# Attention and two expert layers on one core: later softmax sums as reductions with a constant column, an early softplus table, planner constants, and the last output chunk in halves

## The chip, the cores and the metric

The kernel runs on one core of a Trainium2 chip. Its time is the device time of one execution in microseconds; of several runs the median counts. The engines are TensorE (PE in the profile, its weight loads PEld), VectorE (DVE), ScalarE (ACT), GpSimd (POOL) and SyncE (SP), which issues the transfers.

## The reference

Attention over a window of 64 positions is followed by two expert layers, one with softplus and one with a gate.

```python
def _attn_ref(q, k, v):                       # B 4, H 8, S 576, D 64, window 64
    ...
    scores = np.where(mask, scores, -1000000000.0)
    scores = scores - np.max(scores, axis=-1, keepdims=True)
    attn = np.exp(scores)
    attn = attn / (np.sum(attn, axis=-1, keepdims=True) + 1e-09)
    return np.matmul(attn, v).astype(np.float32)

def _moe_ref(x, w_in, w_out):                 # 2304 tokens, 512 -> 2048 -> 512
    h = x @ w_in
    g = np.maximum(h, 0.0) + np.log1p(np.exp(-np.abs(h)))
    return (g @ w_out).astype(np.float32)

def _moe2_ref(x, w_gate, w_val, w_out):       # 2304 tokens, 512 -> 1536 -> 512
    gate = 1.0 / (1.0 + np.exp(-(x @ w_gate)))
    val = x @ w_val
    return (gate * val @ w_out).astype(np.float32)
```

## The kernel before

**Precision.** Every operand of a matmul is kept as a high part (a cast) and a low part (the value less its cast), and a product is three matmuls: high by high, high by low, low by high. So each intermediate result needs a cast on ACT and a subtraction on DVE or POOL before PE can use it. Weights arrive as 64-bit floats and are decoded on the way: `w_load` (L146, a DMA), `w_scale` (L175 or L177, ACT), `w_shift` (L181, DVE), `w_sign` (L186, DVE), `w_low` (L191, DVE), `w_hi` (L197, a cast on ACT) and `w_lo` (L205, DVE or POOL). Where the planner gives `w_scale` the form with Prelu (L175), that also sets the sign, and `w_sign` falls away.

**Stages.** The 2304 tokens are 36 groups of 64 rows. The attention of the first eight groups ("near") is the lead-in, before M1. M1 is the softplus layer in five token blocks of 512, 384, 384, 512 and 512, each with 16 tiles f of the hidden dimension: `m1_proj(b, f)` (L514, twelve matmuls into bank h0 or h1, by f), `m1_act` (L531, softplus on ACT), `g_hi` (L538, ACT), `g_lo` (L544, DVE), and two tiles later `m1_out(b, f)` (L491 to L493, twelve matmuls). Each `m1_proj` or `m1_out` is a slot of PE, some 2.7 us at 512 columns. The attention of block b+1 ("far" in the notes below: all groups from the ninth on) is done during M1 of block b: `att_scores` of a pair of groups (L335, PE), `att_max` (L364, L367, DVE), `att_exp` (L381, ACT, four exponentials of 128x128 with a sum of each row), `att_sum` (L389, L390, DVE), `att_norm` (L397, POOL), then for block 1 `att_transpose` on PE (L413) and `att_copy` (L448), for the later blocks a transpose on DVE and a round trip through DRAM, and at last `att_values` (L474, PE) with its split (L482, L487). M2, the gated layer, follows with its own slots, and ends with `m2_out` (L491 to L493) and `m2_store` (L687 to L694).

**Order.** All engines work in program order. Up to M2 that order comes from `lead_in()`, a list scheduler: of all steps that are ready and could begin within `NEAR` us (`SLACK` after `OPEN`) of the soonest it takes the one with the lowest rank. It works with a table of estimated durations, with the time `OPEN` at which M1 is thought to begin, with `RG` as the distance of two near groups in slots, and with `FETCH`, a time about which it expects transfers to pause. ACT holds one table of functions at a time: exponentials and softplus lie in different ones, and a switch is an `ACT_TABLE_LOAD`. The compiler puts such a load ahead of the first instruction that needs it, and what that instruction waits for is then waited for by the load.

Of the kernel before, what the change touches and what calls it, by code (L numbers as in the profile page):

```python
# [10 lines left out]
F32 = mybir.dt.float32  # L11
# [3 lines left out]
AF = mybir.ActivationFunctionType  # L15
ALU = mybir.AluOpType
AX = mybir.AxisListType
# [3 lines left out]
P = 128  # L21
# [5 lines left out]
FAR = 2  # L27
MERGE = 8
SHIFTED = 2,
RG = 1.2  # L30
HURRY = 1.5
SLACK, NEAR = 0.1, 0.2
STAY = 10.0
FETCH, PAUSE, SAFE = 15.5, 1.4, 0.4
OPEN = 30.0
FLYING, SWITCH, MARGIN, FLIP, LATE = 10, 1.3, 1.1, 8, 0.5
EITHER, HALVES = (("pool", 1.29), ("dve lock", 0.69)), (("pool", 0.75), ("dve lock", 0.42))
COPIES = ("act", 0.55), ("dve", 0.69)
# [10 lines left out]
STB, PB, VB, GB, RB = 3, 2, 2, 3, 2  # L49
# [3 lines left out]
def tile_kernel(ctx: ExitStack, tc: tile.TileContext, qk, vt, w1, w2, wg, wv, wo, out):  # L53
# [20 lines left out]
    nc = tc.nc  # L74
# [8 lines left out]
    NF2 = wg.shape[0]  # L83
    NB1 = len(BLOCKS1)
    N1 = NMAX = max(BLOCKS1)
    NS2 = NT // (2 * HALF)
    NCH = 2 * HALF // P
# [13 lines left out]
    early = main.tile([P, 2, DM], BF16, tag="sums", name="early", bufs=1)  # L101
    ident16, mask16 = (early[:, k, :P] for k in range(2))
    sums = early[:, 0, P:2 * P].bitcast(F32).rearrange("p (g j two) -> p g j two", j=4, two=2)
    x2d = dram.tile([KC, P, NT], F32, tag="x2d", name="x2d")
    wcd = [dram.tile([P, 14 * HC], F32, tag=f"wcd{f}", name=f"wcd{f}") for f in range(NF2)]
    pd = [dram.tile([4, 32, 4, P], F32, tag=f"pd{i}", name=f"pd{i}") for i in range(2)]
# [263 lines left out]
    def att_bias(g, engine):  # L370
        t = st_t[g][:, 0, :]
        eng = nc.gpsimd if engine == "pool" else nc.vector
        eng.tensor_scalar(out=t, in0=t, scalar1=SCALE, scalar2=None, op0=ALU.mult)

    def att_exp(g):
        w = width(g)
        p, st = p_t[g], st_t[g]
        s, scale = ([p[:, j] for j in range(NPAIR)], 1.0) if g >= NG0 else (
            [s_t[g][:, h, j] for h in range(s_t[g].shape[1]) for j in range(NPAIR // s_t[g].shape[1])], SCALE)
        for j in range(NPAIR):  # L380
            nc.scalar.activation(out=p[:, j, :w], in_=s[j][:, :w], func=AF.Exp, bias=st[:, 0, j:j + 1], scale=scale,  # L381
                                 accum_out=sums[:, g, j, :1] if g < NG0 else st[:, 1, j:j + 1])

    def att_sum(g):
        st = st_t[g]
        if g < NG0:
            nc.vector.tensor_reduce(out=st[:, 1, :], in_=sums[:, g], axis=AX.X, op=ALU.add)
        else:
            nc.vector.tensor_scalar(out=st[:, 1, :], in0=st[:, 1, :], scalar1=1e-9, scalar2=None, op0=ALU.add)  # L389
        nc.vector.reciprocal(out=st[:, 2, :], in_=st[:, 1, :])  # L390

    def att_norm(g):
# [135 lines left out]

    def m1_act(b, f):
        t = h_t.pop((b, f))  # L530
        nc.scalar.activation(out=t, in_=t, func=AF.Softplus)  # L531
        u_t[b, f] = t

# [131 lines left out]
    def m2_out(s, f, c):  # L665
        if f == 0 and c == 0:
            acc_t[s] = [psum(f"acc{i}") if i < KC else psum("at", 2) for i in range(NCH)]
        g, w = g_t[s, f, c * P // HALF], w_t["wo", f]
        cols = slice(c * P % HALF, c * P % HALF + P)
        mm3(acc_t[s][c], g[:, 0, cols], g[:, 1, cols], w[:, 0, :], w[:, 1, :], f == 0, f == NF2 - 1)  # L670

    y_t = {}

    def m2_store(s, c):
        t0 = 2 * s * HALF + c * P
        if s < NS2 - 1:
            y = main.tile([P, 512], F32, tag="stage", name="y", bufs=STB)
        elif c % 3:
            y = y_t[c - c % 3][:, c % 3]
        else:  # L680
            y_t[c] = main.tile([P, 4, 512], F32, tag="raw", name="y", bufs=RB)
            y = y_t[c][:, 0]
        if s == NS2 - 1 and c == NCH - 1:
            for k, copy in enumerate((nc.vector.tensor_copy, nc.scalar.copy)):
                cols = slice(256 * k, 256 * k + 256)
                y = y[:, cols] if k == 0 else main.tile([P, 512], F32, tag="stage", name="y", bufs=STB)[:, cols]
                copy(out=y, in_=acc_t[s][c][:, cols])  # L687
                nc.sync.dma_start(out=out[t0:t0 + P, cols], in_=y)
            return
        if c % 2:  # L690
            nc.scalar.copy(out=y, in_=acc_t[s][c])
        else:
            nc.vector.tensor_copy(out=y, in_=acc_t[s][c])
        nc.sync.dma_start(out=out[t0:t0 + P, :], in_=y)  # L694
# [93 lines left out]
    for b in range(1, NB1):  # L788
        s0, s1 = pos[m1_proj, b - 1, 0], pos[m1_proj, b, 0]
        ng, g0 = BLOCKS1[b] // Q, starts1[b] // Q  # L790
        for j in range(ng):
            far = b >= FAR
            first = -5 if far else 5
            t = s0 + first + (s1 - s0 - (14 if far else 12 + first)) * (j // 2) // max(ng // 2 - 1, 1)
            attention(g0 + j, t, far)
            at(t - 4, -60, qk_load, g0 + j)
# [72 lines left out]

    def consts():  # L870
        nc.gpsimd.memset(sums, 1e-9)
        make_identity(nc, ident)
        nc.vector.tensor_copy(out=ident16, in_=ident)
        for t, inside, outside in (mask16, 0.0, -1e30), (mask, 3.0e38, -1e9):
            nc.gpsimd.memset(t, inside)
            for h in range(2):
                m = t[h * Q:(h + 1) * Q, :]
                nc.gpsimd.affine_select(out=m, in_=m, pattern=[[1, P]], compare_op=ALU.is_ge, fill=outside, base=-1,
                                        channel_multiplier=-1)
                nc.gpsimd.affine_select(out=m, in_=m, pattern=[[-1, P]], compare_op=ALU.is_ge, fill=outside, base=Q,  # L880
                                        channel_multiplier=1)
# [198 lines left out]
    def lead_in():  # L1080
# [30 lines left out]
        while todo:  # L1111
            ready, other = [], "soft" if table == "exp" else "exp"
            for n, key in enumerate(todo[:AHEAD]):
# [5 lines left out]
                if all(d in done for d in deps + after[key]):  # L1119
                    ends_at, best = [(done[d] - lead(key, d), made[d]) for d in deps], None  # L1120
                    visit = kind == "pe" and key[0] not in (m1_proj, m1_out) and key[1] >= NG0
                    for kind, us in kind if kind in CHOICES else ((kind, us),):
                        engine, *need = kind.split()
                        start = max([t - (0.08 if e == "pe" else 0.05) * (e == engine) for t, e in ends_at], default=0.0)
                        start = max(free[engine], start + LATE * visit)
                        if engine == "pool" or "lock" in need:
                            start = max(start, held["dve" if engine == "pool" else "pool"])
                        if engine == "sp" and len(flying) >= FLYING:
                            start = max(start, flying[-FLYING])
                        if engine == "act" and need and need[0] != table:  # L1130
                            us += SWITCH
                        if best is None or start + us < best[0] + best[2]:
                            best = start, kind, us
                    ready.append((best[0], rank + FLIP * (best[1].split()[-1] == other) - STAY * (visit and stay is key[0]), n, key,
                                  *best[1:]))
# [95 lines left out]
```

## Time and profile before

| | |
|---|---|
| median of 3 runs | 878.88 us (878.85 to 881.1) |
| the profiled execution | 878.93 us |
| its span | 877.1 us |
| PE busy | 868.3 us, 99% |
| DVE busy | 519.4 us, 59% |
| ACT busy | 395.5 us, 45% |
| first matmul of M1 | at 25.14 us |
| last matmul | begins at 872.46 us |

The profile shows one execution. A busy time is the sum of an engine's instructions, and times in the trace count from the start of the span. A wait is the idle time of an engine just ahead of an instruction, with the instruction of another engine that ended it.

### The profile page before, as it was taken

The page shows a single profiled execution, that of the slowest core. Times are in us where ns is not written, and L with a number is a line of the kernel's source. Part 1 is how long each engine was busy: PE and PEld are TensorE (multiplying, and loading weights), DVE is VectorE, ACT ScalarE, POOL GpSimd, SP SyncE. Part 2 cuts the span into 40 slices and gives each one's busy share as a digit, 9 for nine tenths or more (in the row PEclk, how much of TensorE's full clock was granted, in tenths as well). Part 3 has the DMA queues.
Part 4 walks back from the last instruction along what each step waited for, and adds up shares of the span by engine and source line. Part 5 has one row for each costly group of instructions (what it writes and reads, how often), then busy time and mean ns, then how long its engine had stood idle before and what let it go on. Part 6 is the DMA issues. An engine that isn't in the chain of part 4 may idle for free.

```text
span 877.1 us, 14033 instructions
## 1 busy us (share of the span) xinstructions
PE 868.3 (99%) x5307; PEld 775.3 (88%) x5307; DVE 519.4 (59%) x926; ACT 395.5 (45%) x870; POOL 151.1 (17%) x156
## 2 busy tenths in 40 slices
PE   8999999999999999999999999999999999999998
PEld 5787889999999888888889999999999999999997
DVE  5999985547665654555326677667444448444444
ACT  7878766556566763344323333343222225212222
POOL 5001110112000220012002232332111111111110
PEclk9999999999999999999999999999999999999999
DMA  9955647756877747643325755546554445444442
GB/s 363 390 181 207 207 143 269 246 207 211 263 254 261 266 150 269 199 165 132 133 84 208 269 207 216 217 168 240 208 200 160 151 150 209 168 158 168 169 168 73
DMA packets 56563, 177.73 MB, mean 203 GB/s; under 512 B 6128, under 2 KB 21744, under 8 KB 51888
## 3 DMA queue, kind: packets, MB, share of 16 engines
q1 hardware_dynamic: 56496, 176.84, 56.4%
q8 instruction: 42, 0.69, 0.3%
q14 instruction: 25, 0.20, 0.1%
HBM read 139.59 MB, written 37.22 MB: 202 GB/s over the span
## 4 chain that ended last, share of the span: by engine, by line
PE 93%; ACT 3%; DVE 3%; issue 1%; DMA 1%; POOL 0%; SPq 0%; POOLq 0%; DVEq 0%; ACTq 0%
PE h L514 21%; PE acc L491 11%; PE acc L492 11%; PE acc L493 11%; PE h L491 10%; PE h L493 10%; PE h L492 10%; PE at L493 2%; PE at L492 2%; PE at L491 2%; PE at L474 2%; PE at L335 1%; ACT w L381 1%; DMA w<-in_qk 1%; DVE w L186 1%
## 5 line engine op out<-in xcount | busy, mean ns | idle before, releaser
L514 PE MATMUL h<-xt,w 128*128 128x512 f32 (+1 forms) x960 | 211.6, 369 | 0.9 <-DVE g L544 0.7
L620 DVE TENSOR_TENSOR w<-h,w 128x384 f32<-128x384 f32 x216 | 117.1, 556 | 159.9 <-PE h L493 157.0
L514 PEld LDWEIGHTS h<-xt,w 128*128 128x128 f32 x960 | 174.2, 188 | 25.6 <-DVE g L544 0.9
L491 PE MATMUL h<-w,wc 128*128 128x384 f32 x504 | 169.1, 336 | 0.1
L493 PE MATMUL h<-w,wc 128*128 128x384 f32 x504 | 168.9, 335 | 0.0
L492 PE MATMUL h<-w,wc 128*128 128x384 f32 x504 | 168.7, 335 | 0.0
L632 POOL TENSOR_TENSOR g<-w,g 128x384 fp32r<-128x384 f32 x70 | 74.0, 1057 | 297.0 <-ACT g L625 252.1
L491 PE MATMUL acc<-g,w 128*128 128x512 f32 (+1 forms) x320 | 119.4, 373 | 0.0
L492 PE MATMUL acc<-g,w 128*128 128x512 f32 (+1 forms) x320 | 117.7, 368 | 0.0
L493 PE MATMUL acc<-g,w 128*128 128x512 f32 (+1 forms) x320 | 117.7, 368 | 0.0
L544 DVE TENSOR_TENSOR g<-h,g 128x512 fp32r<-128x512 f32 (+1 forms) x80 | 50.8, 636 | 93.9 <-ACT g L538 87.5
L531 ACT ACTIVATE h<-h 128x512 f32<-128x512 f32 (+1 forms) x80 | 43.0, 540 | 124.2 <-PE h L514 122.2
L491 PEld LDWEIGHTS h<-w,wc 128*128 128x128 f32 x504 | 94.6, 188 | 2.7 <-DVE w L620 0.7
L492 PEld LDWEIGHTS h<-w,wc 128*128 128x128 f32 x504 | 94.6, 188 | 2.0
L493 PEld LDWEIGHTS h<-w,wc 128*128 128x128 f32 x504 | 94.6, 188 | 0.0
L625 ACT CAST g<-w 128x384 fp32r<-128x384 f32 x72 | 36.9, 513 | 118.6 <-DVE w L620 118.6
L491 PEld LDWEIGHTS acc<-g,w 128*128 128x128 f32 x320 | 60.1, 188 | 8.9 <-issue 1.0
L493 PEld LDWEIGHTS acc<-g,w 128*128 128x128 f32 x320 | 60.1, 188 | 7.6
L492 PEld LDWEIGHTS acc<-g,w 128*128 128x128 f32 x320 | 60.1, 188 | 7.1
L397 POOL TENSOR_TENSOR p<-p,st 128x512 f32<-128x512 f32 x28 | 30.7, 1099 | 201.0 <-DVE st L390 114.4
L658 ACT ACTIVATE w<-w 128x384 f32<-128x384 f32 x36 | 19.0, 527 | 94.5 <-DVE w L620 94.4
L493 PE MATMUL acc<-w,g 128*128 128x512 f32 x144 | 56.9, 395 | 0.0
(138 smaller groups left out, 1187.6 us busy)
## 6 DMA issues: line engine op xcount, KB each, us to landing
wc<-wcd SPq DMA_DIRECT2D x36, 1792.0 KB, 7.3
qk<-in_qk SPq DMA_DIRECT2D x28, 512.0 KB, 5.5
wcd<-raw SPq DMA_DIRECT2D x24, 512.0 KB, 3.2
w<-in_w SPq DMA_DIRECT2D x16, 512.0 KB, 8.8
raw<-in_w SPq DMA_DIRECT2D x16, 512.0 KB, 4.9
v<-in_vt SPq DMA_DIRECT2D x25, 256.0 KB, 3.2
raw<-in_wg SPq DMA_DIRECT2D x12, 512.0 KB, 5.3
raw<-in_wv SPq DMA_DIRECT2D x12, 512.0 KB, 6.2
```

The lines of the kernel that those rows point to most:

```text
L397: nc.gpsimd.tensor_tensor(out=p[:, j:j + n, :w], in0=p[:, j:j + n, :w], in1=st[:, 2, j:j + n].unsqueeze(2).to_broadcast([P, n, w]), op=ALU ...
L474: nc.tensor.matmul(out=o[h * Q:(h + 1) * Q, j, k * Q:(k + 1) * Q], lhsT=v[r, (2 * j + h) * Q:(2 * j + h + 1) * Q], rhs=pt, start=True, sto ...
L491: nc.tensor.matmul(out=o, lhsT=lh, rhs=rh, start=first, stop=False)
L492: nc.tensor.matmul(out=o, lhsT=lh, rhs=rl, start=False, stop=False)
L493: nc.tensor.matmul(out=o, lhsT=ll, rhs=rh, start=False, stop=last)
L514: nc.tensor.matmul(out=o, lhsT=w[:, i, kc * P:(kc + 1) * P], rhs=x[:, j, kc, :n], start=t == 0, stop=t == len(turns) - 1)
L531: nc.scalar.activation(out=t, in_=t, func=AF.Softplus)
L544: nc.vector.tensor_tensor(out=g[:, 1, :n], in0=t, in1=g[:, 0, :n].bitcast(F32), op=ALU.subtract)
L620: nc.vector.tensor_tensor(out=out, in0=a, in1=b, op=op)
L625: nc.scalar.copy(out=g[:, 0, :HALF], in_=t)
L632: eng.tensor_tensor(out=g[:, 1, :HALF], in0=t, in1=g[:, 0, :HALF].bitcast(F32), op=ALU.subtract)
L658: nc.scalar.activation(out=sb, in_=u2, func=AF.Sigmoid)
```

## The change

Four parts, and the constants of the planner.

- The sums of the exponentials of the later groups go to a new tile `far_sums`, whose second column holds 1e-9 throughout, and are added up with it by a `tensor_reduce`, as the first eight groups have it already. Before, 1e-9 was added by a `tensor_scalar`.
- The softplus table is asked for by an instruction of its own ahead of the first softplus; the planner lets that step begin 1.3 us (`SWITCH`) earlier.
- The last `m2_out` chunk is done in two halves of 256 columns, three matmuls each. Its two copies are swapped between ACT and DVE, write into one tile, and one transfer of 512 columns sends it.
- The constants change, and block 1's attention is asked for from slot 6 of M1 on, not from slot 5.

```diff
-RG = 1.2
+RG = 1.1
-SLACK, NEAR = 0.1, 0.2
+SLACK, NEAR = 0.15, 0.1
-FETCH, PAUSE, SAFE = 15.5, 1.4, 0.4
-OPEN = 30.0
+FETCH, PAUSE, SAFE = 12.8, 1.4, 0.4
+OPEN = 31.0
...
+    far_sums = main.tile([P, 3, 4, 2], F32, tag="far_sums", name="far_sums", bufs=1)
...
+    def sum_row(g):
+        return sums[:, g] if g < NG0 else far_sums[:, g % 3]
...
-                                 accum_out=sums[:, g, j, :1] if g < NG0 else st[:, 1, j:j + 1])
+                                 accum_out=sum_row(g)[:, j, :1])
...
-        if g < NG0:
-            nc.vector.tensor_reduce(out=st[:, 1, :], in_=sums[:, g], axis=AX.X, op=ALU.add)
-        else:
-            nc.vector.tensor_scalar(out=st[:, 1, :], in0=st[:, 1, :], scalar1=1e-9, scalar2=None, op0=ALU.add)
+        nc.vector.tensor_reduce(out=st[:, 1, :], in_=sum_row(g), axis=AX.X, op=ALU.add)
...
+        if b + f == 0:
+            nc.scalar.preload_act_table(AF.Softplus)
         nc.scalar.activation(out=t, in_=t, func=AF.Softplus)
...
-        mm3(acc_t[s][c], g[:, 0, cols], g[:, 1, cols], w[:, 0, :], w[:, 1, :], f == 0, f == NF2 - 1)
+        n = 256 if (s, f, c) == (NS2 - 1, NF2 - 1, NCH - 1) else 512
+        for k in range(0, 512, n):
+            mm3(acc_t[s][c][:, k:k + n], g[:, 0, cols], g[:, 1, cols], w[:, 0, k:k + n], w[:, 1, k:k + n], f == 0,
+                f == NF2 - 1 and k + n == 512)
...
-            for k, copy in enumerate((nc.vector.tensor_copy, nc.scalar.copy)):
+            for k, copy in enumerate((nc.scalar.copy, nc.vector.tensor_copy)):
                 cols = slice(256 * k, 256 * k + 256)
-                y = y[:, cols] if k == 0 else main.tile([P, 512], F32, tag="stage", name="y", bufs=STB)[:, cols]
-                copy(out=y, in_=acc_t[s][c][:, cols])
-                nc.sync.dma_start(out=out[t0:t0 + P, cols], in_=y)
-            return
-        if c % 2:
+                copy(out=y[:, cols], in_=acc_t[s][c][:, cols])
+        elif c % 2:
             nc.scalar.copy(out=y, in_=acc_t[s][c])
         else:
             nc.vector.tensor_copy(out=y, in_=acc_t[s][c])
         nc.sync.dma_start(out=out[t0:t0 + P, :], in_=y)
...
-            first = -5 if far else 5
+            first = -5 if far else 6
...
+        nc.gpsimd.memset(far_sums, 1e-9)
...
-                        start = max(free[engine], start + LATE * visit)
+                        start = max(free[engine], start + LATE * visit - SWITCH * (key == (m1_act, 0, 0)))
```

Lines behind `far_sums` stand one further down in the changed kernel, those behind the new function two or three further. Each row below is an instruction with its line, its output and inputs, its tile's size, and in brackets the engines or queues whose semaphores it waits for.

**ACT at the start of M1.** This is what ACT does around the first softplus; w and bits are weights being decoded, h the projection's result. Before:

```order
L197 CAST w_481<-bits 128x512 [waits DVE_49]
L175 ACTIVATE bits<-w_289 128x1024 [waits DMAHW3_49,DMAHW2_49]
L531 ACT_TABLE_LOAD [waits PE_49]
L531 ACTIVATE h_523<-h_523 128x512 [waits Activation_49]
L197 CAST w_566<-bits 128x2x512 [waits DVE_49]
L538 CAST g<-h_523 128x512 [waits Activation_49]
```

With the change:

```order
L198 CAST w_483<-bits 128x512 [waits DVE_49]
L176 ACTIVATE bits<-w_327 128x1024 [waits DMAHW3_49,DMAHW2_49]
L533 ACT_TABLE_LOAD
L534 ACTIVATE h_525<-h_525 128x512 [waits PE_49,Activation_49]
L198 CAST w_569<-bits 128x2x512 [waits DVE_49]
L541 CAST g<-h_525 128x512 [waits Activation_49]
```

The wait for PE has moved from the table load to the softplus behind it; the other instructions stand as they did.

**ACT around block 1's first pair of groups.** The exponentials of two groups (p) stand between the softplus of f=3 and that of f=4. Before:

```order
L197 CAST w_670<-bits 128x2x512 [waits DVE_49]
L531 ACTIVATE h_650<-h_650 128x512 [waits PE_49]
L381 ACT_TABLE_LOAD
L381 ACTIVATE p,st<-p,st 128x128 [waits Pool_49]
L381 ACTIVATE p,st<-p,st 128x128 x3
L538 CAST g<-h_650 128x512 [waits Activation_49]
L381 ACTIVATE p,st<-p,st 128x128 [waits DVE_49]
L381 ACTIVATE p,st<-p,st 128x128 x3
L197 CAST w_717<-w_619 128x2x512 [waits DVE_49]
L531 ACT_TABLE_LOAD
L531 ACTIVATE h_693<-h_693 128x512 [waits PE_49]
```

With the change, from the softplus of f=3 on:

```order
L534 ACTIVATE h_648<-h_648 128x512 [waits PE_49]
L541 CAST g<-h_648 128x512 [waits Activation_49]
L198 CAST w_686<-w_622 128x2x512 [waits DVE_49]
L178 ACTIVATE w_665<-w_566 128x1024 [waits DMAHW1_49,DMAHW0_49]
L385 ACT_TABLE_LOAD
L385 ACTIVATE p,far_sums<-p,st 128x128 [waits DVE_49]
L385 ACTIVATE p,far_sums<-p,st 128x128 x3
L385 ACTIVATE p,far_sums<-p,st 128x128 [waits DVE_49]
L385 ACTIVATE p,far_sums<-p,st 128x128 x3
L198 CAST w_760<-w_622 128x2x512 [waits DVE_49]
L534 ACT_TABLE_LOAD
L534 ACTIVATE h_697<-h_697 128x512 [waits PE_49]
```

The cast of g has gone ahead of the exponentials, and a cast of w and a scaling (L178) with it, so that all eight exponentials are in one row.

**DVE around the sums of block 1's second pair.** L389 and L390 are the sum and the reciprocal of a group, in the changed kernel L390 and L391. Before:

```order
L544 TENSOR_TENSOR g<-h_844,g 128x512 [waits Activation_49]
L191 SCALAR_TENSOR_TENSOR w_801<-raw,w_801 128x1024
L186 SCALAR_TENSOR_TENSOR w_801<-raw,w_801 128x1024 [waits DMAHW7_49,DMAHW6_49]
L181 TENSOR_SCALAR w_908<-w_908 128x1024 [waits Activation_49]
L389 TENSOR_SCALAR st<-st 128x4 [waits Activation_49]
L390 RECIPROCAL st<-st 128x4 [waits DVE_49]
L191 SCALAR_TENSOR_TENSOR w_801<-raw,w_801 128x1024
L389 TENSOR_SCALAR st<-st 128x4 [waits Activation_49]
L390 RECIPROCAL st<-st 128x4 [waits DVE_49]
```

With the change:

```order
L547 TENSOR_TENSOR g<-h_865,g 128x512 [waits Activation_49]
L182 TENSOR_SCALAR w_818<-w_818 128x1024
L187 SCALAR_TENSOR_TENSOR w_818<-raw,w_818 128x1024 [waits DMAHW5_49,DMAHW4_49,DVE_49]
L206 TENSOR_TENSOR w_886<-w_665,w_886 128x512
L192 SCALAR_TENSOR_TENSOR w_818<-raw,w_818 128x1024 [waits DVE_49]
L182 TENSOR_SCALAR w_818<-w_818 128x1024
L390 TENSOR_REDUCE st<-far_sums 128x4 [waits Activation_49]
L391 RECIPROCAL st<-st 128x4 [waits DVE_49]
L390 TENSOR_REDUCE st<-far_sums 128x4 [waits Activation_49]
L391 RECIPROCAL st<-st 128x4 [waits DVE_49]
```

The additions are reductions over `far_sums` now, and the two sums stand next to each other, where an operation of the weights' decoding (L191) stood between them.

On PE the same 31 visits to attention stand between the slots of M1 as before. Counted in slots of M1 that are done ahead of a visit, the transposes of block 1's first pair move from 12 to 10, the scores of its second pair from 13 to 12, the values of the first pair from 14 to 15; the transposes of the second pair stay at 16, later ones move by one or two, or not. In the lead-in, SP's first 22 transfers keep their places; on PE one pair's values (L474) move ahead of group 7's scores, on ACT one cast (L482) ahead of group 6's exponentials, on POOL the normalisation of group 4 ahead of a copy. Of the sign operations (L186) four are left out, since four more scalings are in the Prelu form (L175 before, L176 now); four more subtractions (L246, the low parts of M2's combined weights) go to POOL. The number of table loads is the same, 15. At the end ACT's copy waits for the last of the six matmuls, DVE's copy for ACT's, and the transfer for DVE's.

## Rows read from the trace of the kernel before

**Rows 1.** The page: busy time, share of the span and instructions by engine.

```profile
PE 868.3 (99%) x5307; PEld 775.3 (88%) x5307; DVE 519.4 (59%) x926; ACT 395.5 (45%) x870; POOL 151.1 (17%) x156
```

**Rows 2.** Windows: stretch, length, busy us (instructions) of PE, PEld, DVE, ACT, POOL, clock, DMA.

```profile
9.30:20.90 11.60, 10.53 (x173) 7.74 (x171) 9.34 (x31) 11.60 (x57) 8.53 (x11) 1.00 1.04 402
26.00:100.00 74.00, 72.67 (x460) 58.74 (x459) 71.30 (x105) 61.31 (x112) 7.81 (x6) 1.00 0.66 240
100.00:870.00 770.00, 769.93 (x4529) 699.62 (x4528) 428.88 (x768) 312.31 (x674) 130.29 (x121) 1.00 0.55 193
```

**Rows 3.** Waits of PE by their releaser: total us, times, longest.

```profile
PE h L514 <- DVE g L544: 0.7, 1, 0.7
PE at L413 <- POOL p L397: 0.6, 1, 0.6
```

**Rows 4.** Timeline around M1's first softplus: start, us, engine, line, operation, [idle before].

```profile
26.53 1.16 ACT L175 ACTIVATE bits<-w 128x1024 f32<-128x1024 f32 x1
...
28.20 1.28 ACT L531 ACT_TABLE_LOAD   x1 [0.52 <-PE h L514]
28.99 1.23 DVE L191 SCALAR_TENSOR_TENSOR bits<-w,bits 128x1024 uint32<-128x1024 uint32 x1
29.49 0.58 ACT L531 ACTIVATE h<-h 128x512 f32<-128x512 f32 x1
...
30.92 0.59 ACT L538 CAST g<-h 128x512 fp32r<-128x512 f32 x1
...
31.67 0.68 DVE L544 TENSOR_TENSOR g<-h,g 128x512 fp32r<-128x512 f32 x1
...
32.41 0.97 PE L514 MATMUL h<-xt,w 128*128 128x512 f32 x3 [0.74 <-DVE g L544]
```

**Rows 5.** The sums by their source lines: duration least/median/most in ns, first and last start.

```profile
L389 DVE TENSOR_SCALAR st<-st x28: 126/170/1008, 49.8 to 323.9; 128x4 f32<-128x4 f32 x28
L387 DVE TENSOR_REDUCE st<-early x8: 130/150/161, 7.4 to 19.3; 128x4 f32<-128x8 f32 x8
```

**Rows 6.** Timeline around block 1's second pair of groups, POOL, DVE and PE.

```profile
72.31 1.84 POOL L397 TENSOR_TENSOR p<-p,st 128x512 f32<-128x512 f32 x1 [19.91 <-DVE st L390]
...
73.17 1.01 DVE L389 TENSOR_SCALAR st<-st 128x4 f32<-128x4 f32 x1
...
74.56 1.04 POOL L397 TENSOR_TENSOR p<-p,st 128x512 f32<-128x512 f32 x1 [0.41 <-DVE st L390]
...
75.66 0.55 PE L413 MATMUL at<-ident,p 128*128 128x128 f32 x3 [0.59 <-POOL p L397]
```

**Rows 7.** Timeline of ACT around block 1's first exponentials.

```profile
39.79 1.05 ACT L197 CAST w<-bits 128x1024 fp32r<-128x1024 f32 x1 [1.93 <-DVE bits L191]
...
48.73 0.58 ACT L531 ACTIVATE h<-h 128x512 f32<-128x512 f32 x1
```

**Rows 8.** Timelines of DVE and PE around the softplus of f=4.

```profile
50.85 0.69 DVE L544 TENSOR_TENSOR g<-h,g 128x512 fp32r<-128x512 f32 x1 [0.38 <-ACT g L538]
...
54.30 2.88 PE L514 MATMUL h<-xt,w 128*128 128x512 f32 x12
```

**Rows 9.** Timeline of the end of the kernel.

```profile
872.22 0.40 PE L492 MATMUL at<-w,g 128*128 128x512 f32 x1
...
872.46 0.40 PE L493 MATMUL at<-w,g 128*128 128x512 f32 x1
872.89 0.42 DVE L687 COPY y<-at 128x256 f32<-128x256 f32 x1
873.34 0.90 SPq L688 DMA_DIRECT2D out_y<-y  x2
873.35 0.37 ACT L687 COPY y<-at 128x256 f32<-128x256 f32 x1 [1.26 <-DVE y L687]
```

**Rows 10.** Transfers of the output: KB each, median us from issue to landing.

```profile
out_y<-y SPq DMA_DIRECT2D x17, 256.0 KB, 2.2
...
out_y<-y SPq DMA_DIRECT2D x2, 128.0 KB, 2.1
```

## The prediction

> **What bounds the kernel now.** The page's line of busy times comes first: TensorE (PE) is busy for 868.3 us of the span, no other engine for more than 59% of it [rows 1]. The profiled execution took 878.93 us, its span 877.1, so 1.83 us lie outside the span; the median of the runs shown is 878.88, so a sum made against 878.93 can be read against the runs as it stands. What a measurement of this kernel can tell from no change is about 0.3%, 2.6 us. A change that leaves PE's work as it is can take only PE's idle time, 8.8 us in all, and the next views say where that is.
>
> The busy times by stretch [rows 2]: from 100 to 870 us PE is busy 769.93 of 770.00, so nothing is to be had there. From 26 to 100 us it is idle for 1.33 us. In the lead-in (9.3 to 20.9) it is idle for 1.07 us, but ACT is busy for the whole 11.60 us: that stretch ends when ACT has done its work. The clock granted to PE is 1.00 of its upper level in all three, so the clock is no term here. The list of PE's waits names the two idle times of the second stretch: 0.7 us in which a projection waits for DVE's split of a softplus result (L544), 0.6 us in which a transpose of block 1 waits for POOL's normalisation (L397) [rows 3]. They make up the 1.33 us. What is left lies at the start and, some 4.2 us, behind the last matmul.
>
> **The softplus table.** The timeline at M1's start [rows 4] reads as a chain. ACT's decoding operation ends at 26.53 + 1.16 = 27.69; its next instruction is the table load, which begins at 28.20, after 0.52 us in which ACT waits for PE. Softplus comes at 29.49, the cast of its result at 30.92, DVE's split at 31.67, and PE goes on at 32.41, having waited 0.74. The change asks for the table ahead of the wait: the order of ACT shows the load without a wait and the wait for PE on the Softplus instead. Then the load lies in 27.69 to 28.97, Softplus begins near 28.98 instead of 29.49, and cast and split follow as densely as now. Is something else late next? The w cast between Softplus and the g cast needs a DVE operation that is over before the one that begins at 28.99, so it moves too. So the wait falls from 0.74 to about 0.24: **-0.50**. Bounds: 0 if the load waits all the same, -0.74 if the wait vanishes.
>
> On what a switch costs, the trace has 1.28 for the load and Softplus 0.01 us behind it (28.20 + 1.28 = 29.48) [rows 4]. The Trainium skill ("ScalarE: Activation LUTs", section "What ACT_TABLE_LOAD costs") puts 1.28 us for the load and about 1.38 us of drain on every switch. The trace agrees on the load and shows no drain behind it. By that rule, with the drain ahead of an early load, the load would begin at an estimated 29.07, later than now, and this term would be nothing; that is one of the rivals below.
>
> **The sums of the later groups.** 28 additions of a constant (L389) become 28 reductions over a pair of columns. The one takes 126/170/1008 ns (least, median, most), the eight reductions that the first block has already take 130/150/161 [rows 5]. Median against median that is 0.02 us less for each, all of it on DVE, which is not what PE waits for. The longest ones matter: the addition at 73.17 takes 1.01 us, and lies beside a POOL normalisation of 1.84 that began at 72.31; the next normalisation begins at 74.56, and PE's transposes wait for it until 75.66, of which 0.59 us are idle [rows 6]. A reduction of 0.15 would end the sum 0.86 earlier, but POOL itself is not free before 72.31 + 1.84 = 74.15, so the second normalisation gains 0.41 by that alone. The new order also puts these scores one slot of M1 earlier (12 slots done instead of 13 when the pair's scores begin), and a slot is some 2.7 us of PE. PE's transposes keep their place at the 16th slot, so the normalisation should be over when PE comes: **-0.59**. Bounds: -0.41 (the shorter sum alone) and 0.
>
> The Trainium skill ("SBUF — State Buffer", section on who interferes with whom) says that tensor_scalar can take the port that DVE shares with GpSimd for a whole instruction and that tensor_reduce never does on this chip. The rows of 1.01 us beside POOL's 1.84 agree with the first half [rows 6]; that no reduction was above 161 ns agrees with the second [rows 5]. The sum above needs only those rows.
>
> **The order of M1.** The constants of the planner change what the greedy list takes next. In the lead-in all 22 first DMAs keep their places, one pair's values move ahead of the last scores on PE, one cast moves ahead of an exponential on ACT. ACT has the same work there and is busy throughout [rows 2], so I put that at **0**, with bounds of +-0.3 by the smaller waits of PE before M1. In M1 all 31 visits of PE to attention stay; of the visits of block 1 and of the last blocks some move by one or two slots, which costs PE nothing as long as data are there. Four of the decoders' sign operations on DVE vanish, since ACT does them with its scaling; a DVE operation of that kind and size takes 1.23 (the L191 at 28.99) [rows 4], so DVE has 4.9 us less, in a stretch in which it is busy for 71.30 of 74 us [rows 2]. POOL takes over four subtractions later on, where it is idle most of the time. All of this lies beside PE: **0**.
>
> What the new order does bring is a longer row of work on ACT between two Softplus. Before, ACT went from Softplus of f=3 into eight exponentials and back to Softplus of f=4 at 48.73. Now a scaling of 1.16 [rows 4] and a w cast of 1.05 [rows 7] stand ahead of the exponentials: 2.21 more. DVE's split of that Softplus ended at 50.85 + 0.69 = 51.54, and the projection which takes over its bank began at 54.30 [rows 8]: 2.76 us to spare, so 0.55 are left. I cost it at nothing, and it is the narrowest cover of the change.
>
> **The end.** The last chunk's three matmuls of 512 columns become six of 256. Two of 512 begin 0.24 us apart (872.22, 872.46); six halves take +0 if each takes half of that and +0.72 if each takes as long as a whole. I take +0.05, since the columns are the same in number. The two copies were one after the other (DVE 0.42 from 872.89, ACT 0.37 from 873.35), and ended at 873.72 [rows 9]. As built, ACT's copy waits for the sixth matmul and DVE's for ACT's, so they stay one after the other; the split of the matmuls gives nothing to overlap. The second transfer went out behind the second copy, and the single one will do the same. It is of 256 KB instead of 128: 2.2 against 2.1 from issue to landing [rows 10]: +0.1. SP no longer has another transfer's issue in hand (its two took 0.90 from 873.34) when the last copy ends, -0.1. Sum **+0.05**, bounds -0.42 (one copy hidden) and +0.8.
>
> **Sum.** -0.50 - 0.59 + 0 + 0.05 = -1.04, so 878.93 - 1.04 = 877.9 us.
>
> **The rivals.**
> (a) The waits are only moved. For: from 26 to 100 us DVE is busy for 71.30 of 74 us [rows 2], so PE, arriving a half microsecond earlier, can meet weights that are not split yet. Against: four DVE operations go away there. Half of the 1.09 given back is 878.4, all of it 878.9 to 879.0. Chance 0.18, at 878.6.
> (b) Slower: the row of exponentials on ACT. If ACT has to wait once in its longer row for DVE, as it did for 1.93 us at 39.79 [rows 7], Softplus of f=4 comes 1.93 - 0.55 = 1.38 us too late, and PE's projection of f=6 stands. That gives -1.04 + 1.38, 879.3. It decides from a wait of 1.6 us in that row on, where it has eaten the whole gain. For: the casts in it need DVE's results. Against: DVE has less to do. Chance 0.14.
> (c) The lead-in shortens: the waits of PE in it are worth up to 0.6, of which one cast moved ahead on ACT could free some. ACT's full 11.60 us speak against it. 877.4. Chance 0.08.
> (d) The early table does not help, since the load waits for the engine to be empty or the engine's own waits stay: only the sums' 0.59 is left, 878.4. The trace speaks against it, since the load followed its wait at once. Chance 0.08.
> (e) The reductions of half columns overlap at the end after all: 877.5. Chance 0.04.
>
> **How the numbers follow.** The forecast, both waits gone or nearly so, has 0.48 and stands at 877.9, with 877.5 to 878.3 as its own range. Rivals (a) and (d) reach up to 878.9, (b) to 879.3, (c) and (e) down to 877.4. Nothing among the rows gives more than 1.33 + 0.6 + 0.42 = 2.35 us, that is 876.6, and the bound of the six matmuls with rival (b) gives 880.0. The range from 877.1 to 879.3 leaves out about 2 in 10. Nearly all of it is within 2.6 us of 878.9: faster by over 0.3% (below 876.3) 0.03, slower by over 0.3% (above 881.5) 0.05, for a chain like (b) at both switches, within 0.3% 0.92.
>
> **What would show it.** In the changed kernel's profile the table load of M1's start begins near 27.7, right behind the scaling, and Softplus near 29.0; PE's wait for L544 is 0.2 to 0.3. No sum of 28 takes more than 0.2 us, and PE's wait for POOL's L397 is gone from the list of waits. PE's idle time from 26 to 100 us falls from 1.33 to some 0.3. At the end the two copies are still one after the other, and from the last matmul to the end it is 4.2 us as now. The prediction is wrong if PE shows a new wait for ACT or DVE between 45 and 60 us, if M1's first projection moves by over 0.3, or if the six halves take markedly longer than 0.7 us together.

## The result

The changed kernel took 889.66 us (median of 5 runs, 889.57 to 889.80), the kernel before 878.90 (878.85 to 881.10): a ratio of 1.0117, 95% interval 1.0103 to 1.0132. It is slower by 10.8 us, where 877.9 was forecast, and outside the range of 877.1 to 879.3.

**The profile after.** The page of the changed kernel, span and busy times, answers to [rows 1]:

```profile
span 887.8 us, 14026 instructions
PE 880.8 (99%) x5310; PEld 779.5 (88%) x5310; DVE 514.5 (58%) x917; ACT 398.3 (45%) x871; POOL 156.7 (18%) x161
```

PE is busy for 12.5 us more, with three instructions more. Its idle time is 7.0 us, less than the 8.8 of before. So the loss is no wait. The list of PE's waits of the changed kernel, which answers to [rows 3], says the same: the two waits of before are gone from it, and none is new that matters.

```profile
PE s L505 <- DVE idle L503: 1.0, 1, 1.0
PE t L414 <- ACT pt L449: 0.4, 1, 0.4
PE t L414 <- POOL w L398: 0.3, 1, 0.3
```

The same stretches of the changed kernel as in [rows 2]:

```profile
9.30:20.90 11.60, 10.41 (x173) 7.61 (x170) 9.51 (x31) 11.60 (x57) 8.76 (x11) 1.00 1.04 402
26.00:100.00 74.00, 73.93 (x461) 58.86 (x460) 66.19 (x101) 62.74 (x113) 6.89 (x6) 1.00 0.66 242
100.00:870.00 770.00, 769.93 (x4473) 693.39 (x4472) 422.80 (x752) 311.42 (x669) 135.90 (x124) 1.00 0.55 193
```

What the reader is to see is the number in brackets behind PE's busy time. From 100 to 870 us PE is busy for 769.93 us in both kernels, at a clock of 1.00 in both, and gets through 4529 matmuls before and 4473 after. From 390 to 450 us, the middle of M1's last block with little attention in it, it is 266 before,

```profile
390.00:450.00 60.00, 60.00 (x266) 49.71 (x265) 26.95 (x42) 23.88 (x43) 5.58 (x5) 1.00 0.28 97
```

and 259 with the change:

```profile
390.00:450.00 60.00, 60.00 (x259) 48.27 (x258) 27.96 (x43) 25.59 (x46) 7.33 (x6) 1.00 0.32 114
```

Each matmul takes longer. The timelines show it in the starts of neighbouring matmuls, 0.22 to 0.23 us apart before:

```profile
404.69 0.39 PE L493 MATMUL acc<-g,w 128*128 128x512 f32 x1
404.91 0.39 PE L491 MATMUL acc<-g,w 128*128 128x512 f32 x1
405.14 0.39 PE L492 MATMUL acc<-g,w 128*128 128x512 f32 x1
405.37 0.39 PE L493 MATMUL acc<-g,w 128*128 128x512 f32 x1
```

and 0.23, 0.24, 0.23 apart with the change:

```profile
404.83 0.40 PE L494 MATMUL acc<-g,w 128*128 128x512 f32 x1
405.06 0.39 PE L492 MATMUL acc<-g,w 128*128 128x512 f32 x1
405.30 0.39 PE L493 MATMUL acc<-g,w 128*128 128x512 f32 x1
405.53 0.40 PE L494 MATMUL acc<-g,w 128*128 128x512 f32 x1
```

Taken over the stretch from 400 to 440 us in nanoseconds, the starts of before are 226.7 apart without exception (226 or 227), those after 231, 232 and 237 in turn, 233.3 in the mean. The matmuls of 384 columns of M1's second and third block go from 173.3 to 176.7 in the mean, counted from the twelfth matmul behind each visit to attention on.

**What the change asked for did happen.** The timeline of the changed kernel at M1's start, which answers to [rows 4]:

```profile
26.43 1.15 ACT L176 ACTIVATE bits<-w 128x1024 f32<-128x1024 f32 x1
...
27.60 1.28 ACT L533 ACT_TABLE_LOAD   x1
...
28.90 0.58 ACT L534 ACTIVATE h<-h 128x512 f32<-128x512 f32 x1
...
31.07 0.68 DVE L547 TENSOR_TENSOR g<-h,g 128x512 fp32r<-128x512 f32 x1
...
31.81 1.23 PEld L515 LDWEIGHTS h<-xt,w 128*128 128x128 f32 x6 [0.21 <-DVE g L547]
```

The load follows the scaling at once. Softplus comes 0.59 us earlier, 0.48 of it counted from the end of the scaling. PE's weight load waits 0.21 where it waited 0.88 before, and PE's matmul behind it, which waited 0.74 [rows 4], less than 0.1. The sums, by their source line, are 120 to 163 ns where 1008 was the longest [rows 5], and around the second pair of groups [rows 6] no wait is left:

```profile
L390 DVE TENSOR_REDUCE st<-far_sums x28: 120/161/163, 49.9 to 327.2; 128x4 f32<-128x8 f32 x28
```

```profile
71.60 2.04 POOL L398 TENSOR_TENSOR p<-p,st 128x512 f32<-128x512 f32 x2 [18.44 <-DVE st L390]
...
74.64 1.04 PE L414 MATMUL at<-ident,p 128*128 128x128 f32 x8
```

**Where the new tile lies.** `far_sums` takes 96 bytes of each partition and is made behind `early`, ahead of the other tiles of its pool. As built, xt, g, wc and all tiles behind them stand 96 bytes higher than before; the weights w, in a pool ahead of it, stand where they were. Before, the first bytes of w, xt and g were all 128 past a multiple of 256. With the change xt and g differ from w by 96. In M2 the roles are exchanged, w being the moving columns and wc and g2 (the gated results) the weights that PE holds, so the difference there, columns less weights and modulo 256, is 160.

### The profile page after: what moved, and what is told of

Read it like the earlier page. It is cut to its first block, busy times and chain, and to the rows that moved or that the text cites. A ratio compares the mean times of both kernels' runs of the same rounds, so it can differ in the third digit from the quotient of the medians.

```text
span 887.8 us, 14026 instructions
## 1 busy us (share of the span) xinstructions
PE 880.8 (99%) x5310; PEld 779.5 (88%) x5310; DVE 514.5 (58%) x917; ACT 398.3 (45%) x871; POOL 156.7 (18%) x161
## 4 chain that ended last, share of the span: by engine, by line
PE 96%; ACT 2%; DMA 1%; DVE 1%; issue 0%; POOL 0%; SPq 0%
PE h L515 22%; PE acc L492 12%; PE acc L494 11%; PE acc L493 11%; PE h L492 10%; PE h L494 10%; PE h L493 10%; PE at L494 2%; PE at L492 2%; PE at L493 2%; PE at L475 2%; PE at L336 1%; ACT w L385 1%; DMA w<-in_qk 1%; PE at L414 0%
## 5 line engine op out<-in xcount | busy, mean ns | idle before, releaser
L515 PE MATMUL h<-xt,w 128*128 128x512 f32 (+1 forms) x960 | 216.5, 374 | 0.2
L492 PE MATMUL acc<-g,w 128*128 128x512 f32 (+1 forms) x320 | 120.4, 376 | 0.0
L494 PE MATMUL acc<-g,w 128*128 128x512 f32 (+1 forms) x320 | 119.6, 374 | 0.0
L493 PE MATMUL acc<-g,w 128*128 128x512 f32 (+1 forms) x320 | 118.9, 372 | 0.0
```

The costliest lines, as they stand in the source:

```text
L492: nc.tensor.matmul(out=o, lhsT=lh, rhs=rh, start=first, stop=False)
L493: nc.tensor.matmul(out=o, lhsT=lh, rhs=rl, start=False, stop=False)
L494: nc.tensor.matmul(out=o, lhsT=ll, rhs=rh, start=False, stop=last)
L515: nc.tensor.matmul(out=o, lhsT=w[:, i, kc * P:(kc + 1) * P], rhs=x[:, j, kc, :n], start=t == 0, stop=t == len(turns) - 1)
```

## The experiments

Theory A: a matmul's pace depends on the offset between its two operands' addresses, and the 96 bytes moved one against the other. Rival B: the new order or the added instructions slow PE.

| run | what it is | median us | before beside it | ratio, 95% interval |
|---|---|---|---|---|
| e1_sums_last | the change, new tile behind PE's | 876.84 | 879.12 | 0.9974 (0.9965 to 0.9984) |
| e2_before_96 | before, unused tile of 96 bytes | 889.74 | 879.12 | 1.0121 (1.0108 to 1.0135) |
| e3_after_64 | the change, tile of 64 bytes | 884.81 | 879.12 | 1.0066 (1.0052 to 1.0080) |
| e4_const_96 | the change, tile ahead of w too | 877.32 | 879.12 | 0.9981 (0.9972 to 0.9990) |
| p1_no_table | e1 without the early table | 877.46 | 879.05 | 0.9980 (0.9971 to 0.9988) |
| p2_old_sums | e1 with the sums of before | 877.01 | 879.05 | 0.9972 (0.9962 to 0.9982) |
| p3_old_order | e1 with the constants of before | 879.18 | 879.05 | 1.0000 (0.9991 to 1.0009) |
| p4_old_tail | e1 with the end of before | 877.45 | 879.05 | 0.9979 (0.9970 to 0.9987) |
| x1_before_32 | before, unused tile of 32 bytes | 886.94 | 878.99 | 1.0090 (1.0075 to 1.0105) |
| x2_order_only | before, new constants alone | 877.93 | 878.99 | 0.9988 (0.9979 to 0.9996) |
| x3_table_only | before, early table alone | 878.42 | 878.99 | 0.9995 (0.9986 to 1.0004) |

**The tile behind everything that PE reads (e1_sums_last).**

```diff
-    far_sums = main.tile([P, 3, 4, 2], F32, tag="far_sums", name="far_sums", bufs=1)
+    far_t = []
...
+        if not far_t:
+            far_t.append(late["apool"].tile([P, 3, 4, 2], F32, tag="far_sums", name="far_sums", bufs=1))
+            nc.gpsimd.memset(far_t[0], 1e-9)
+        return far_t[0][:, g % 3]
...
-        nc.gpsimd.memset(far_sums, 1e-9)
```

> The whole change, but the new sums' tile of 96 bytes a partition is made in the last pool, behind all tiles that PE reads, so that these stand at the addresses that they have in the kernel before. Theory A (the 96 bytes push the projections' and the outputs' operands off a 64-byte boundary, and each matmul that reads them takes some 6.7 ns more): the matmuls of 512 columns are 227 ns apart again and the time is 877.9 us, what the forecast's other terms give. Rival B (the new order or the added instructions slow PE): 889.6, as with the change.

876.84 us: the loss is gone, and the rest of the change gives 2.3 us, twice the forecast's 1.0. From 390 to 450 us PE does 267 matmuls:

```profile
390.00:450.00 60.00, 60.00 (x267) 49.67 (x266) 25.43 (x40) 23.39 (x42) 5.28 (x5) 1.00 0.28 97
```

**The tile alone in the kernel before (e2_before_96).**

```diff
+    spare = main.tile([P, 24], F32, tag="spare", name="spare", bufs=1)
...
+        nc.gpsimd.memset(spare, 1e-9)
```

> The kernel before with an unused tile of 96 bytes a partition at the place where the change has its sums, and nothing else. Theory A: the matmuls of 512 columns are 233 ns apart, and the time is 889 to 891 us (889.7 and the 1 us that the rest of the change gives). Rival B: 878.9, as before.

889.74 us, as slow as the whole change, from a tile that nothing reads. Rival B falls. The same stretch:

```profile
390.00:450.00 60.00, 60.00 (x259) 48.28 (x258) 27.26 (x42) 26.15 (x47) 7.84 (x6) 1.00 0.34 118
```

**64 bytes (e3_after_64).**

```diff
-    far_sums = main.tile([P, 3, 4, 2], F32, tag="far_sums", name="far_sums", bufs=1)
+    far_sums = main.tile([P, 2, 4, 2], F32, tag="far_sums", name="far_sums", bufs=1)
...
-        return sums[:, g] if g < NG0 else far_sums[:, g % 3]
+        return sums[:, g] if g < NG0 else far_sums[:, g % 2]
```

> The whole change with two rows of sums for three, so that the tile takes 64 bytes a partition. Theory A with a boundary of 64 bytes: 877.9 us. Theory A with a boundary of 128 bytes: about 889, or half of the loss. Rival B: 889.6.

884.81 us. A boundary of 64 bytes is not what counts. M1's matmuls of 512 columns are 228.9 ns apart (again from the twelfth behind a visit on), those of 384 columns 173.3 as before. The stretch has 263 matmuls:

```profile
390.00:450.00 60.00, 60.00 (x263) 49.20 (x263) 26.44 (x41) 23.40 (x43) 6.30 (x5) 1.00 0.28 97
```

Most of this loss lies in M2. Against e1_sums_last it is 8.0 us; by the mean distances in the two traces an estimated 3.6 us of it come from M2's 1512 products of 384 columns (2.4 ns each), 2.6 from its 648 outputs (4.0 each) and 1.8 from M1's 1152 matmuls of 512 columns (1.6 each).

**Weights and activations moved alike (e4_const_96).**

```diff
-    far_sums = main.tile([P, 3, 4, 2], F32, tag="far_sums", name="far_sums", bufs=1)
+    far_sums = const.tile([P, 3, 4, 2], F32, tag="far_sums", name="far_sums", bufs=1)
```

> The whole change with the 96 bytes in the first pool, ahead of the weights, so that weights and activations are all moved by 96 bytes alike. Theory A by absolute addresses: at least 889.6 us, more if the weights' offset costs too. Theory A by the offset between a matmul's two operands: 877.9. Rival B: 889.6.

877.32 us. xt and g stand at the very addresses that they have in the slow kernel, and the loss is gone, since w moved with them. It is the offset between the two operands; my first form of the theory, a boundary for each operand, is refuted. That this run is 0.48 us longer than e1_sums_last was not looked into. The stretch has 266 matmuls again:

```profile
390.00:450.00 60.00, 60.00 (x266) 49.73 (x265) 25.96 (x41) 23.40 (x42) 5.85 (x5) 1.00 0.28 97
```

**TensorE by itself (m1_offsets).** The kernel is a list of rows of 48 matmuls, each with its own offsets, in bytes, of the weights (wo_) and the columns (xo):

```python
        for n, wo_, xo in PAIRS:
            a, c = wo_ // 4, xo // 4
            for t in range(COUNT // 3):
                o = acc[t // 4 % 4][:, :n]
                k = t % 4 * P
                for i, j in ((0, 0), (0, 1), (1, 0)):
                    nc.tensor.matmul(out=o, lhsT=wr[:, a + 1024 * i + k:a + 1024 * i + k + P],
                                     rhs=xr[:, c + 1024 * j:c + 1024 * j + n],
                                     ...
```

> No part of the computation: TensorE alone does rows of 48 matmuls of 128x128 weights by 512 or 384 columns of one constant, in the kernel's pattern of high and low parts, each row with its own offsets of the weights' and the columns' first address, in bytes past a multiple of 128. No other engine works meanwhile. Theory A (the offset between the two operands): 226.7 ns from matmul to matmul where both offsets are the same (0 and 0, 32 and 32, 64 and 64, 96 and 96) and where they differ by 128 or 256; about 229 at a difference of 64 and 233 at 96. Rival C (only the columns' own offset counts): 233 at 96 and 96 too, 226.7 where only the weights are moved. Rival D (it is other engines' or the transfers' traffic that the offset brings into conflict): 226.7 everywhere.

One run of it. Two windows of its trace, in rows with a difference of 32 and of 256; behind the length stand PE, PEld, DVE and POOL (ACT has no instruction), the clock and the transfers:

```profile
17.30:27.30 10.00, 10.00 (x45) 8.03 (x44) 0.00 (x0) 0.00 (x0) 1.00 0.01 2
95.50:105.50 10.00, 10.00 (x46) 8.28 (x45) 0.00 (x0) 0.00 (x0) 1.00 0.00 0
```

From the starts in the trace, mean ns from matmul to matmul in a row, from the seventh on. The row at a difference of 0 stands twice in the list; the first began at 427 ns from matmul to matmul, ahead of the trace's first record of the clock, so the value is that of its repetition at the end. Differences above 128 at 384 columns were made by moving the weights.

```text
columns' offset less weights', mod 256      0     32     64     96    128    160    192    224
512 columns                             226.8  233.3  228.8  233.4  233.4  234.2  233.4  233.3
384 columns                             173.3  173.3  173.3  176.7      -  176.6  174.7  173.3
both operands at 32, 64 or 96, 512 columns: 226.7, 226.8, 226.8;  columns at 256, weights at 0: 226.7
columns at 16, weights at 0, 512 columns: 231.6
```

Rivals C and D fall: equal offsets give the full pace whatever they are, and no other engine is at work. An offset of 128, which I had expected to be free, costs as much as 96; of the differences tried, at 512 columns only 0 and 256 cost nothing. At the kernel's 96 and 64 it gives what the full kernels show in M1: 233.4 and 176.7 against 233.3 and 176.7, 228.8 and 173.3 against 228.9 and 173.3.

**32 bytes (x1_before_32).** As e2_before_96, with 8 columns for 24.

> The kernel before with an unused tile of 32 bytes a partition where the change has its sums. Theory A with the rows of matmuls alone as its measure (512 columns 233.3 ns at a difference of 32, 384 columns 173.3 as without): the 1152 projections and outputs of 512 columns in the first layer cost 1152 x 6.6 ns = 7.6 us, the 648 outputs of the second layer up to 648 x 6.6 = 4.3, all others nothing: 886.5 to 891 us, most likely 889, as much as 96 bytes although it is a third of them. Rival, the loss grows with the shift: 879.0 + 10.6 / 3 = 882.5.

886.94 us: a third of the bytes costs 7.95 of 10.6 us. M1's matmuls of 512 columns take 233.3 ns, as the row by itself does; those of 384 columns 174.4, about 1 ns more than the row. The 889 was somewhat high, the proportional 882.5 is refuted.

**The parts, with the addresses right.** Each of four takes one part out of e1_sums_last. They ran on another chip, on which before took 879.05 where it had taken 879.12 beside e1_sums_last. Differences of 0.6 us are small: the intervals of the ratios overlap. What speaks for them is that the slowest run of e1_sums_last (876.73 to 877.21) is faster than the fastest of p1_no_table (877.26 to 877.72) and of p4_old_tail (877.35 to 877.65), and that the traces show a place for each.

p1_no_table, without the early request for the table:

```diff
-        if b + f == 0:
-            nc.scalar.preload_act_table(AF.Softplus)
...
-                        start = max(free[engine], start + LATE * visit - SWITCH * (key == (m1_act, 0, 0)))
+                        start = max(free[engine], start + LATE * visit)
```

> The whole change with the sums' tile in the last pool (876.84 us), without the early request for the softplus table and without its term in the planner. By the forecast's first term: the wait ahead of the third projection is back at 0.7 and the time is 0.5 longer, 877.3. Rival, the weights bound that place: 876.8.

877.46 us, 0.62 longer, with the wait for DVE's split back in the list of PE's waits:

```profile
PE h L520 <- DVE g L550: 0.7, 1, 0.7
```

p2_old_sums, with the additions of before:

```diff
-                                 accum_out=sum_row(g)[:, j, :1])
+                                 accum_out=sums[:, g, j, :1] if g < NG0 else st[:, 1, j:j + 1])
...
-        nc.vector.tensor_reduce(out=st[:, 1, :], in_=sum_row(g), axis=AX.X, op=ALU.add)
+        if g < NG0:
+            nc.vector.tensor_reduce(out=st[:, 1, :], in_=sums[:, g], axis=AX.X, op=ALU.add)
+        else:
+            nc.vector.tensor_scalar(out=st[:, 1, :], in0=st[:, 1, :], scalar1=1e-9, scalar2=None, op0=ALU.add)
```

> The same version (876.84 us) with the sums of the later groups by tensor_scalar as before, without the added tile. By the forecast's second term: some of the 28 sums take 0.4 to 1.0 us again, and PE's transposes wait 0.3 to 0.6 us for POOL: 877.1 to 877.4. Rival, the new order alone took that wait away: 876.8.

877.01 us, 0.17 longer, which the spread of the runs (876.73 to 877.21 and 876.82 to 878.10) doesn't tell from nothing. The forecast's step falls: with the new order the wait is gone from this run's list too, so the reductions are not what took it away.

p3_old_order, with the planner's constants of before:

```diff
-RG = 1.1
+RG = 1.2
-SLACK, NEAR = 0.15, 0.1
+SLACK, NEAR = 0.1, 0.2
-FETCH, PAUSE, SAFE = 12.8, 1.4, 0.4
+FETCH, PAUSE, SAFE = 15.5, 1.4, 0.4
-OPEN = 31.0
+OPEN = 30.0
...
-            first = -5 if far else 6
+            first = -5 if far else 5
```

> The same version (876.84 us) with the planner's constants and block 1's first slot as before. The forecast put the order at nothing, so 876.8 to 877.2. Rival, the order gave what the forecast's two waits don't explain of the gain of 2.3 us: 878.0 (876.84 and some 1.2).

879.18 us: with the old constants the other parts together give nothing. The timeline of this run has a new wait, which takes back what they brought:

```profile
47.56 1.86 POOL L403 TENSOR_TENSOR p<-p,st 128x512 f32<-128x512 f32 x1 [26.24 <-DVE st L396]
...
48.44 2.13 DVE L206 TENSOR_TENSOR w<-w,w 128x512 fp32r<-128x512 f32 x2
50.02 2.56 PE L520 MATMUL h<-xt,w 128*128 128x512 f32 x10 [1.40 <-DVE w L206]
```

Two of DVE's subtractions take 2.13 us beside a POOL normalisation of 1.86, and PE waits 1.40 for weights. The Trainium skill ("SBUF — State Buffer", section on who interferes with whom) says that a DVE instruction with two inputs in SBUF contends with a GpSimd instruction that reads SBUF; this row agrees with it (two of the same operation take 1.28 us at 47.50 in the kernel before, with no POOL instruction beside them).

This run also has the reductions without the new order, and so shows what they are worth at the second pair of groups. Before, the two normalisations took 3.29 us with the gap of 0.41 between them (72.31 to 75.60) [rows 6]; in the timeline of this run they begin at 72.17, stand without a gap and take 3.30. The shorter sum brought POOL's end nothing, where the forecast counted 0.41 for it alone.

The fourth, p4_old_tail, puts back the end of before:

> The same version (876.84 us) with the last chunk whole, its copies and its two transfers as before. By the forecast: no difference (876.8, within 0.1). Rival, by the trace of the version, in which the time from the last matmul's start to the end is shorter than before: 0.3 longer, 877.1.

877.45 us, 0.61 longer. The rival had the direction right and half of the size. The timeline of this run's end (its span is 875.6 us),

```profile
870.72 0.39 PE L499 MATMUL at<-w,g 128*128 128x512 f32 x1
871.14 0.42 DVE L695 COPY y<-at 128x256 f32<-128x256 f32 x1
871.59 1.17 SPq L696 DMA_DIRECT2D out_y<-y  x2
871.60 0.37 ACT L695 COPY y<-at 128x256 f32<-128x256 f32 x1 [1.23 <-DVE y L695]
```

and that of e1_sums_last (875.1 us):

```profile
870.87 0.28 PE L499 MATMUL at<-w,g 128*128 128x256 f32 x1
...
871.19 0.37 ACT L697 COPY y<-at 128x256 f32<-128x256 f32 x1 [0.81 <-PE at L499]
871.59 0.42 DVE L697 COPY y<-at 128x256 f32<-128x256 f32 x1 [0.41 <-ACT y L697]
```

The last copy ends at 871.97 in the one and 872.01 in the other. From there to the end it is 3.6 us with two transfers and 3.1 with one; SP is at work on its two issues for 1.17 us, from 871.59: the second begins at 872.43, where the only one of e1_sums_last begins at 872.04.

**Two parts alone in the kernel before.** x2_order_only has the constants of the diff above the other way round:

> The kernel before with the new constants and block 1's first slot alone: table, sums and tail as before. If the parts add up (0.62 for the table, 0.17 for the sums, 0.61 for the tail, above 876.84): 878.2. If the order needs the others to give anything: 879.0.

877.93 us, 1.06 faster, nearer to the sum of the parts. Its timeline around the second pair of groups has no wait ahead of the transposes, with the sums still by tensor_scalar:

```profile
71.25 0.14 DVE L389 TENSOR_SCALAR st<-st 128x4 f32<-128x4 f32 x1
71.42 0.18 DVE L390 RECIPROCAL st<-st 128x4 f32<-128x4 f32 x1
71.51 2.04 POOL L397 TENSOR_TENSOR p<-p,st 128x512 f32<-128x512 f32 x2 [17.66 <-DVE st L389]
74.36 1.03 PE L413 MATMUL at<-ident,p 128*128 128x128 f32 x8
```

One sum of the 28 still takes 1.01 us in this run, at 51.15; no wait of PE in its list comes of it.

x3_table_only adds the early request and no term in the planner:

```diff
         t = h_t.pop((b, f))
+        if b + f == 0:
+            nc.scalar.preload_act_table(AF.Softplus)
         nc.scalar.activation(out=t, in_=t, func=AF.Softplus)
```

> The kernel before with the early request for the softplus table alone, no term in the planner, so that all other instructions stand where they stood. By the forecast's first term: PE's wait ahead of the third projection falls from 0.7 to 0.3, and the time is 878.5. Rival (a) of the forecast, the half microsecond is given back at the next weights: 878.9 to 879.1, with a wait for DVE's L205 in the profile.

878.42 us, 0.57 faster by the medians, as the forecast's first term has it; its interval still holds 1. The waits for DVE's split and for L205 are not in its list. The trace is of its slowest execution (879.53), in which M1 begins 1.3 us late, so it shows the wait gone and not the time.

## Why the prediction was wrong

**The step that failed** is the sentence that a change which leaves PE's work as it is can take only PE's idle time. The forecast costed the new tile's instructions and put no cost on its 96 bytes. They moved xt, g and wc against w, and PE's own work grew though its instructions stayed. Between the changed kernel and e1_sums_last, which differ by little more than the place of that tile, lie 12.8 us. Followed along the starts, 8.4 us of them arise up to the 1860th of M1's 1920 matmuls of projections and outputs (it begins 6.97 us later than before in the one, 1.46 earlier in the other), the rest behind it, most of it in M2, whose outputs of 512 columns go from 229.3 ns in the mean before to 233.8. None of the five rivals had it; a range made from waits could not hold it.

**The softplus table** was right: forecast -0.50, wait 0.2 to 0.3; found 0.57 alone and 0.62 among the rest, the wait of the weight load 0.21. The estimate that hung on a drain of 1.38 us did not come true: the load began 0.02 us after the scaling's end (26.43 + 1.15 = 27.58, load at 27.60) and Softplus 0.02 behind it.

**The sums and the order.** The wait of 0.59 did go, but for the other reason: the new order brings scores and sums forward, and the reductions add 0.17, which the runs don't tell from nothing. The forecast had counted the earlier scores in for its -0.59, but gave 0.41 of it to the shorter sum alone; p3_old_order shows none of that. The size was off too: from the weight load of the first of the eight transposes to that of the projection behind them it was 1.80 us before (74.24 to 76.04) and 0.99 in x2_order_only, so 0.81. The order is worth 1.06 alone, where the forecast put it at nothing and booked its gain to the sums; where the other 0.25 arise was not looked into.

**Rival (a)**, gain given back at DVE's weights, is what p3_old_order showed, and not the changed kernel. From 26 to 100 us DVE is busy for 66.19 of 74 us in the changed kernel, 5.1 less than before, where 4.9 were forecast; it is 67.19 in x2_order_only and 70.86 in p3_old_order, so the new order is what provides that. **Rival (b)** did not come: no wait of PE for ACT between 45 and 60 us. **Rival (c)** did not either: M1's first projection begins at 25.07 us, at 25.14 before. **Rivals (d) and (e)** fall with the early table, which helped, and with the two copies, which did not overlap.

**The end.** +0.05 was forecast, -0.6 found. The copies stayed one after the other, as forecast; the term mis-sized was the single transfer, which I held for longer by its bytes (2.2 against 2.1) when it spares the second issue behind the first. With the addresses right the parts come to 2.3 us: 0.6 the table, 0.6 the end, about 1.1 the order and the sums.

**What stays open**: why a difference of the addresses costs time, and why it has this pattern. M2 does not follow the rows throughout. Its products of 384 columns take 0.7 ns more with the change than in e1_sums_last and 2.4 more with 64 bytes, where the rows by themselves gave 3.3 for a difference of 160 and 1.4 for one of 192. And its outputs of 512 columns are 229.3 ns apart in the kernel before, at a difference of 0: of each eighteen, the first nine take 224 to 236 and the other nine about 227. They stand behind products of 384 columns, and the row of m1_offsets that follows one of 384 columns begins in the same way (from its second distance on 224, 231, 236, 228, 232, 231, then 227). So the table's values are those of a row that has settled, and short rows cost something without any difference; what causes that was not looked into.

## What to carry to other kernels

Where a change adds a tile, print the addresses of TensorE's operands before and after: keep weights and moving columns at the same offset modulo 256 bytes (shown here for operands of 4 bytes an element, 128x128 weights and 384 or 512 columns), by putting a small tile behind them all, or ahead of both. Where a kernel is slower without a new wait, count matmuls in a stretch in which TensorE is busy throughout: the same busy time with fewer instructions is a slower TensorE, which no list of waits shows. And take parts of a change out one at a time: here a gain of 2.3 us was hidden under a loss of 12.8.

## What the runs showed of the hardware that I had not expected

At a granted clock of 1.00, TensorE's pace in a settled row depends on where weights and columns lie towards each other. It is 226.7 to 226.8 ns for 512 columns when the addresses differ by 0 or 256 bytes, 228.8 at 64, and 233.3 to 234.2 at the other multiples of 32 below 256. For 384 columns it is 173.3 up to a difference of 64, and 176.7 at 96. It does so with no other engine at work (m1_offsets), and an unused tile of 96 bytes cost a whole kernel 10.6 us by it (e2_before_96).
